# One 130-column product for the high and low parts of the values in three of four output slots, with the two halves added by VectorE

## The chip, the core and the metric

The kernel runs on one core of one Trainium2 chip. The metric is device microseconds of one execution, from the host's view of the device; the core's own span, from the first to the last profiled instruction, is a little shorter. TensorE (PE in the rows; PEld is its weight load) does the matmuls, VectorE (DVE), ScalarE (ACT) and GpSimd (POOL) the elementwise work, SyncE (SP) issues nearly all DMAs. The engines run side by side and wait for each other through semaphores.

## The reference

Attention over 4 batches, 8 heads, 768 positions and head dimension 64, with a block mask of 32 x 32 blocks (neighbours, first and last block, three sampled blocks for each row of blocks), and behind it a two-layer MLP with a mish-like gate:

```python
scores = scale * np.matmul(q, k.transpose(0, 1, 3, 2))      # (4, 8, 768, 768)
scores = np.where(mask, scores, -1e9)
attn = np.exp(scores - np.max(scores, axis=-1, keepdims=True))
attn = attn / (np.sum(attn, axis=-1, keepdims=True) + 1e-09)
x = np.matmul(attn, v)                                       # then (3072, 512)
h = x @ w_in                                                 # (3072, 2048)
g = h * np.tanh(np.where(h > 20.0, h, np.log1p(np.exp(np.minimum(h, 20.0)))))
return g @ w_out                                             # (3072, 512)
```

All is float32 (the weights come as float64). In the kernel most products are float16: a value is split into a high part (its float16 rounding) and a low part (the rest), and a product of two such values is three float16 products, high x high, high x low and low x high.

## The kernel before

A row of blocks has 32 queries. Two neighbouring rows of blocks make a job; the first and the last row of each batch, which see all 768 keys, are a job of one row each ("dense"). So a batch has 13 jobs: 11 of two rows and 2 dense ones, 52 in all. The first batch (jobs 0 to 12) is computed in float32 ("exact"), the other three in float16 parts; the change concerns these 39 jobs alone.

One job goes through these steps, each a task in the code of `attend`:

- S (L657): scores of 32 queries x 4 head pairs against 256 gathered keys for each row and each of two heads (`g`), into PSUM.
- L700, L713, L726: row maximum (DVE), its negative scaled (ACT or DVE), exponential (ACT).
- T (L746): 128 x 128 transposes of the exponentials, four for each group of 256 keys; L763 (ACT) writes their high part and L766 (DVE) their low part, the tile `pp`.
- O (L801): exponentials times values. The values lie in SBUF (`vg`, `v`, `vt`) as 130 columns for each key and head: 64 high parts, a one, 64 low parts, a zero. The 65th column gives the sum of the exponentials. For each row of a job (`w`), each head of a pair (`g`) and each half of the 256 keys (`k`) there are three products: high exponentials x high values and the one (65 columns), high x low values (64 columns), low exponentials x high values (65 columns). Each is four matmuls, one for each head pair, on a tile of 128 rows x 32 columns of the array, which write to the four quarters of the PSUM partitions. All three add up in the same 65 columns of PSUM. The pool `o` has one buffer.
- L824, L825, L827 (DVE, one task): small constant added to the sum, reciprocal, product, into the tile `xs` in SBUF.
- X (L834): `xs` transposed, 128 columns for each row; L852 (ACT) and L855 (DVE) make the high and low part of the MLP's input.

The MLP works on 256 tokens at a time (12 such groups): H (L1033) is `x @ w_in` in pieces of 12 matmuls of 256 columns; L1042 to L1079 on ACT, DVE and POOL make the gate; Y (L1093) is the product with `w_out` in pieces of 6 matmuls of 512 columns.

The order of all engines' instructions is made when the program is built, by `Plan.emit`: a list scheduler that takes each task's written duration (the second argument of `add`), its dependencies, the buffers of each pool and a priority (`key`), and puts the tasks one by one. The MLP's pieces on TensorE have a fixed order and come where nothing else of the attention is due. A task that names a second engine under `also` goes to the one that would end it sooner. The written durations decide the order and nothing else: on the chip the engines run that order and wait for semaphores.

Of the kernel before, what the change touches and what calls it, by code (L numbers as in the profile page):

```python
# [13 lines left out]
AF = mybir.ActivationFunctionType  # L14
ALU = mybir.AluOpType
# [6 lines left out]
PSC = 4096.0  # L22
# [4 lines left out]
             xs=2, hs=3, us=3, g=4, ys=1, kt=1, q=2, ssk=2, ssv=2, ssq=2, sck=2, scv=2, scq=2, iv=2, ns=3, ws=2,  # L27
# [13 lines left out]
class Plan:  # L41
# [10 lines left out]
    def add(self, eng, dur, fn, r=(), w=(), new=(), use=(), key=0.0, lat=0.0, kind=None, port=False, also=()):  # L52

        t = Task({eng: (dur, fn, port), **{e: (d, f, port) for e, d, f in also}}, key, lat, new, kind, len(self.tasks))
        self.tasks.append(t)
        for ring, k in new:
            self.first[k], self.users[k] = t, []
        for k in r:
            t.deps.update(self.writer.get(k, ()))
            self.readers.setdefault(k, []).append(t)  # L60
        for k in w:
            t.deps.update(self.writer.get(k, ()))
            t.deps.update(self.readers.pop(k, ()))
# [122 lines left out]
def attn_mish_kernel(ctx: ExitStack, tc: tile.TileContext, qT, kT, v, sampled, blocks, w_in, w_out, out):  # L186
# [11 lines left out]
    nc = tc.nc  # L198
    P = 128
    B, NPR, D2, S = qT.shape  # L200
    D = D2 // 2
# [15 lines left out]
    VW = 2 * D + 2  # L217
# [7 lines left out]
    exact = lambda b: b == 0  # L225
# [436 lines left out]
    def attend(job):  # L662

        b, i, sus, nt, dense = job["b"], job["i"], job["sus"], job["nt"], job["dense"]
        nsu = len(sus)
        W2 = S - 512
        ks, kmx, kp, ko = ("s", i), ("mx", i), ("pt", i), ("o", i)
# [4 lines left out]
        def s_fn():  # L672
# [15 lines left out]
            r=KT3(b) + [("q", b, t) for t in qts] + (["t in order"] if dense else [(k, su["ng"] % NKG) for su in sus for k in ("kg", "kw")]),  # L688
            w=[ks, ("begun", i), "s in order"] + (k2 if dense else []), new=[("s", ks)] + ([("t", k) for k in k2] if dense else []),
# [18 lines left out]
        def nb_fn(eng):  # L708
            mx, nb = tl[kmx], new(sb, "nb", ("nb", i), [P, 2, 2])
            for w in wq:  # L710
                ns = ns0 if exact(b) else tl["ns", b, sus[w.start]["qb"] // TB]
                if eng == "ACT":
                    nc.scalar.activation(out=nb[:, :, w], in_=mx[:, :, w], func=AF.Copy, scale=ns[:, 1:2])  # L713
                else:
                    nc.vector.tensor_scalar(out=nb[:, :, w], in0=mx[:, :, w], scalar1=ns[:, 1:2], scalar2=None,
                                            op0=ALU.mult)
        add("ACT", 0.25 * len(wq), lambda: nb_fn("ACT"), r=[kmx] + NS, w=[("nb", i)],
            new=[("nb", ("nb", i))], key=45.5 + (0 if b == 0 else -20), also=[("DVE", 0.35 * len(wq), lambda: nb_fn("DVE"))])
# [16 lines left out]
        for n in range(2):  # L735
            add("ACT", 1.7 if dense and n == 0 else 1.15, lambda n=n: ex_fn(n),
                r=[kmx, ("nb", i), ks] + (k2 if dense else []) + NS,
                w=[("p", i, n)], new=[("pt", k) for k in kps] if n == 0 else (), use=kps, key=-1.5 + (-3 if b == 0 else 7))
# [15 lines left out]
        def pp_fn(j, eng):  # L754
            pp_new(j)
            if eng == "ACT":
                nc.scalar.activation(out=tl["p32", i, j], in_=tl["t", i, j], func=AF.Copy)
            else:
                nc.vector.tensor_copy(out=tl["p32", i, j], in_=tl["t", i, j])
# [9 lines left out]
        for j in range(nt):  # L769
            kj = ("t", i, j)  # L770
            add("PE", 0.62 if exact(b) else 0.48, lambda j=j: t_fn(j), r=[("p", i, j // 2 if dense else j)], w=[kj, "t in order"], new=[("t", kj)], use=kps,
                key=-8 + (-40 if b == 0 else 24), lat=0.25, kind=("T", i))
            kpp = ("pp", i, j)
            if exact(b):
                add("ACT", 0.62, lambda j=j: pp_fn(j, "ACT"), r=[kj], w=[("ph", i, j), ("pl", i, j)], use=[kpp],
                    new=[("pp", kpp)], key=-9.5, also=[("DVE", 0.72, lambda j=j: pp_fn(j, "DVE"))])
# [2 lines left out]
            add("DVE", 0.72, lambda j=j: pl_fn(j), r=[kj, ("ph", i, j)], w=[("pl", i, j)], use=[kpp], key=11.5)  # L779

        def o_fn(j):
            if j == 0:
                new(ps["o"], "o", ko, [P, 2, 2, D + 2])
            o, w = tl[ko], 0 if dense else j
            vt = (vg32 if exact(b) else vgs)[sus[w]["ng"] % NVG] if not dense else tl["vt", b, j] if sus[0]["qb"] else tl["v", b, j]
            if exact(b):
                for g in range(2):
                    for k in range(2):
                        for c in range(NPR):
                            cs = slice(c * BS, (c + 1) * BS)  # L790
                            nc.tensor.matmul(  # L791
                                o[cs, w, g, 0:D + 1], tl["p32", i, j][:, k, g, cs], vt[:, k, 2 * c + g],
                                start=j == 0 and g == 0 and k == 0, stop=j == nt - 1 and g == 1 and k == 1)
                return
            hi, lo = tl["ph", i, j], tl["pl", i, j]
            for g in range(2):
                for k in range(2):
                    for n, (p, v0, v1) in enumerate(((hi, 0, D + 1), (hi, D + 1, 2 * D + 1), (lo, 0, D + 1))):
                        for c in range(NPR):
                            cs = slice(c * BS, (c + 1) * BS)  # L800
                            nc.tensor.matmul(  # L801
                                o[cs, w, g, 0:v1 - v0], p[:, k, g, cs], vt[:, k, 2 * c + g, v0:v1],
                                start=j == 0 and g == 0 and k == 0 and n == 0,
                                stop=j == nt - 1 and g == 1 and k == 1 and n == 2)
        def rv(j):
            if not dense:
                return ("vg", sus[j]["ng"] % NVG)
            if sus[0]["qb"]:
                return ("vg", j) if j < NVG else ("vt", b)
            return ("v", b, j)  # L810

        for js in [[j] for j in range(nt)] if i < SPLIT else [list(range(nt))]:
            add("PE", (0.68 if exact(b) else 0.46) * len(js), lambda js=js: [o_fn(j) for j in js],
                r=[k for j in js for k in (("ph", i, j), ("pl", i, j), rv(j))], w=[ko, "o in order"],
                use=[("pp", i, j) for j in js],
                new=[("o", ko)] if js[0] == 0 else (), key=-1 + (-33 if b == 0 else -9), lat=0.25, kind=("O", i))

        def xs_fn():
            o = tl[ko]
            r = new(sb, "r", ("r", i), [P, nsu, 2])  # L820
            if exact(b):
                nc.vector.tensor_scalar(out=r, in0=o[:, 0:nsu, :, D], scalar1=1e-9, scalar2=iv_r, op0=ALU.add, op1=ALU.mult)
            else:
                nc.vector.tensor_scalar(out=r, in0=o[:, 0:nsu, :, D], scalar1=PSC * 1e-9, scalar2=None, op0=ALU.add)  # L824
            nc.vector.reciprocal(out=r, in_=r)  # L825
            xs = new(sb, "xs", ("xs", i), [P, nsu, 2, D])
            nc.vector.tensor_tensor(  # L827
                out=xs, in0=o[:, 0:nsu, :, 0:D], in1=r.unsqueeze(3).to_broadcast([P, nsu, 2, D]), op=ALU.mult)
        add("DVE", 0.8, xs_fn, r=[ko] + ([("sc", "v", b, 0)] if exact(b) else []), w=[("r", i), ("xs", i)], new=[("r", ("r", i)), ("xs", ("xs", i))], key=39.5 + (0 if b == 0 else -27))

        def tx_fn():
            tx = new(ps["t"], "t", ("tx", i), [P, nsu, P])
# [21 lines left out]
        def xl_fn():  # L854
# [3 lines left out]
            new=[("x" + n, ("x" + n, b, t)) for t in fresh for n in "hl"], use=kx, key=-19.5 + (0 if b == 0 else -39))  # L858
# [279 lines left out]
    def open_mlp():  # L1138
# [7 lines left out]
        key=-1025)  # L1146
    load32("k", 0)
    load32("q", 0)
    for j in T3:
        load(0, "v", [j])  # L1150
    add("ACT", 1.0, lambda: which(new), w=["off", "z"],
        new=[("raw", ("z",))], key=-1, lat=6.0)
# [9 lines left out]
    for k in range(NFP):  # L1162
# [3 lines left out]
        key=-3)  # L1166
# [26 lines left out]
    for i, job in enumerate(jobs):  # L1193
        b, o = job["b"], i % JB
# [4 lines left out]
        for su in job["sus"]:  # L1199
# [5 lines left out]
            elif su["qb"]:  # L1205
                fetch_dense(su)
                fresh = jobs[i + 1]["sus"][0]["ng"]
        attend(job)
        if i == LAST:
            add("PE", 0.0, spare.clear, r=["zeros", ("begun", i)], use=[("zeros",)], key=-982)  # L1210
# [27 lines left out]
    at = {"done": 0.0, "next": 0.0, "job": 0, "last": None, "shape": None}  # L1238
# [73 lines left out]
```

## Time and profile before

| | us |
|---|---|
| median of 3 runs | 766.79 (765.13 to 769.03) |
| the profiled execution | 768.72 |
| its span | 766.7 |
| TensorE busy | 733.4 (96%) |
| ScalarE busy | 535.8 (70%) |
| VectorE busy | 504.0 (66%) |
| GpSimd busy | 230.6 (30%) |

The profiled execution is 2.0 us longer than its span and 1.9 us longer than the median. Attention runs until about 642 us; the rest of the span is MLP alone. The steps O of the three float16 batches lie between 203 and 642 us. A row of a timeline merges equal instructions that follow each other; its duration goes to the end of the last one, which overlaps the start of the next row, so that the time that a step takes is read from the start of its row to the start of the next one.

### The profile page before, as it was taken

Reading aid. Unit: us, or ns where it says so; the run is one execution under the profiler, and the core shown is the slowest. Engines: PE = TensorE matmul, PEld = TensorE weight load, DVE = VectorE, ACT = ScalarE, POOL = GpSimd, SP = SyncE. Lnnn points to the kernel's source line nnn. Section 1 sums busy time; section 2 is a strip of 40 time slices with the busy share of each in tenths; the row PEclk is TensorE's granted clock in tenths of the full one; section 3 lists DMA queues with packets and bytes.
Section 4 is the critical chain, followed back from the end, with each engine's and each line's share of the span. In section 5 each row is a group of like instructions: output and inputs, shape, how many; then the busy total and the mean of one; then the engine's idle time right before and its main releaser. Section 6 shows DMA issues by size and latency. Waiting matters only on the chain.

```text
span 766.7 us, 28001 instructions
## 1 busy us (share of the span) xinstructions
PE 733.4 (96%) x11905; PEld 507.3 (66%) x11905; DVE 504.0 (66%) x891; ACT 535.8 (70%) x864; POOL 230.6 (30%) x327
## 2 busy tenths in 40 slices
PE   9777898999999999999999999999999999999998
PEld 3554676766677766677767776766776666666663
DVE  3886897887888748859676676777855454425241
ACT  2556787989887867888797678877864655455650
POOL 2363423585645422514340113234522100000000
PEclk9999999999999999999999999999999999999999
DMA  7987768442346533543363336233233221000000
GB/s 263 363 222 219 232 210 230 147 128 87 106 120 168 160 96 110 170 123 105 103 210 97 94 100 200 84 97 101 71 92 90 96 67 48 15 15 15 15 15 27
DMA packets 55904, 94.07 MB, mean 123 GB/s; under 512 B 8035, under 2 KB 18788, under 8 KB 55780
## 3 DMA queue, kind: packets, MB, share of 16 engines
q1 hardware_dynamic: 55584, 92.03, 40.0%
q8 instruction: 93, 1.52, 0.8%
q14 instruction: 31, 0.25, 0.1%
q10 hardware_dynamic: 196, 0.27, 0.1%
HBM read 79.32 MB, written 12.95 MB: 120 GB/s over the span
## 4 chain that ended last, share of the span: by engine, by line
PE 82%; DMA 9%; DVE 4%; issue 2%; SPq 2%; ACT 1%; ACTq 0%; POOL 0%
PE y L1093 31%; PE h L1033 30%; PE t L746 6%; PE o L801 5%; PE s L657 4%; DMA wr<-in_moe_w_in_dram 3%; DMA vg<-vd 3%; PE tx L834 2%; PE o L791 1%; DMA wor<-in_moe_w_out_dram 1%; DMA kt<-in_k_dram 1%; PE s L647 1%; PE zeros L868 1%; DMA raw_q<-in_q_dram 1%; DVE us L1060 1%
## 5 line engine op out<-in xcount | busy, mean ns | idle before, releaser
L1033 PE MATMUL h<-xh,wi 128*128 128x256 f16 x1536 | 285.3, 274 | 0.0
L1093 PE MATMUL y<-wo,g 128*128 128x512 f16 x1152 | 277.7, 379 | 1.5 <-issue 1.5
L1033 PEld LDWEIGHTS <-wi 128*128 128x128 f16 x2304 | 224.7, 99 | 52.4 <-issue 1.5
L1033 PE MATMUL h<-xl,wi 128*128 128x256 f16 x768 | 210.5, 274 | 0.0
L1093 PEld LDWEIGHTS <-g 128*128 128x128 f16 x1152 | 111.0, 98 | 101.2 <-issue 3.2
L585 POOL COPY kg<-kt 128x256 f16 (+1 forms) x222 | 97.6, 485 | 145.6 <-PE s L657 115.8
L1042 ACT ACTIVATE hs<-h,gsc 128x512 f32<-128x512 f32 x96 | 65.6, 683 | 63.7 <-PE h L1033 62.9
L726 ACT ACTIVATE pt<-s,nb,ns 128x256 f32<-128x256 f32 (+1 forms) x208 | 105.7, 580 | 5.1 <-PE t L746 3.1
L1066 DVE SCALAR_TENSOR_TENSOR hs<-us,hs 128x1024 f32<-128x1024 f32 x48 | 59.6, 1242 | 43.1 <-ACT us L1065 43.1
L700 DVE TENSOR_REDUCE mx<-s 128x4 f32<-128x1024 f32 x44 | 53.7, 1221 | 31.5 <-PE s L657 30.1
L1077 POOL TENSOR_TENSOR g<-hs,g 128x1024 f16<-128x1024 f32 x19 | 42.3, 2229 | 98.9 <-ACT g L1072 60.2
L746 PE MATMUL t<-ident,pt 128*128 128x128 f32 x448 | 69.5, 278 | 2.0 <-ACT pt L726 1.7
L1062 POOL TENSOR_TENSOR us<-us 128x1024 f32<-128x1024 f32 x22 | 43.4, 1971 | 74.7 <-DVE us L1060 72.2
L766 DVE SCALAR_TENSOR_TENSOR pp<-t,pp 128x512 f16<-128x512 f32 x84 | 56.1, 681 | 11.6 <-ACT pp L763 11.5
L763 ACT ACTIVATE pp<-t 128x512 f16<-128x512 f32 x84 | 48.3, 590 | 17.7 <-PE t L746 13.7
L746 PEld LDWEIGHTS t<-ident,pt 128*128 128x128 f32 x448 | 50.8, 141 | 13.9 <-ACT pt L726 3.2
L1056 ACT ACTIVATE us<-hs,hsc 128x1024 f32<-128x1024 f32 x48 | 55.1, 1149 | 1.5
L1064 ACT ACTIVATE us<-us 128x1024 f32<-128x1024 f32 x48 | 50.7, 1056 | 4.9 <-POOL us L1062 4.1
L1065 ACT ACTIVATE us<-us 128x1024 f32<-128x1024 f32 x48 | 50.7, 1056 | 0.7
L1060 DVE TENSOR_SCALAR us<-us 128x1024 f32<-128x1024 f32 x48 | 36.5, 760 | 21.7 <-ACT us L1056 21.5
L801 PEld LDWEIGHTS <-pp 128*32 128x32 f16 x4032 | 37.2, 94 | 13.7 <-issue 12.3
L852 ACT ACTIVATE xh<-tx 128x256 f16<-128x256 f32 (+1 forms) x60 | 19.4, 337 | 31.4 <-PE tx L834 24.8
(194 smaller groups left out, 849.7 us busy)
## 6 DMA issues: line engine op xcount, KB each, us to landing
vg<-vd SPq DMA_DIRECT2D x304, 65.0 KB, 2.3
vg<-vd SPq DMA_DIRECT2D x80, 195.0 KB, 2.9
wr<-in_moe_w_in_dram SPq DMA_DIRECT2D x8, 1024.0 KB, 9.2
wor<-in_moe_w_out_dram SPq DMA_DIRECT2D x16, 512.0 KB, 5.0
vd<-v SPq DMA_DIRECT2D x12, 520.0 KB, 3.4
raw_v<-in_v_dram SPq DMA_DIRECT2D x12, 512.0 KB, 5.7
out_dram<-ys SPq DMA_DIRECT2D x24, 256.0 KB, 2.1
raw_q<-in_q_dram SPq DMA_DIRECT2D x9, 512.0 KB, 5.5
```

The costliest lines, as they stand in the source:

```text
L585: nc.gpsimd.tensor_copy(out=dst, in_=src)
L700: nc.vector.tensor_reduce(out=mx.rearrange("p g w -> p (g w)"), in_=tl[ks].rearrange("p g (w k) -> p (g w) k", k=KT), axis=AX.X, op=ALU.max)
L726: ex = lambda o, x, g, w: nc.scalar.activation(out=o, in_=x, func=AF.Exp, bias=nb[:, g, w:w + 1], scale=ns(w)[:, 0:1])
L746: nc.tensor.transpose(t[:, k, g], src, ident)
L766: nc.vector.scalar_tensor_tensor(out=tl["pl", i, j], in0=tl["t", i, j], scalar=PSC, in1=tl["ph", i, j], op0=ALU.mult, op1=ALU.subtract)
L801: nc.tensor.matmul(o[cs, w, g, 0:v1 - v0], p[:, k, g, cs], vt[:, k, 2 * c + g, v0:v1], start=j == 0 and g == 0 and k == 0 and n == 0, stop ...
L1033: nc.tensor.matmul(h[:, f2].rearrange("p (s q) -> p s q", q=BS), wi[:, fp, w, cc, fs], x[:, :, cc], start=f2 == 0 and k == 0, stop=f2 == 1 ...
L1042: nc.scalar.activation(out=tl[kq][:, 2 * (fp % 2):2 * (fp % 2) + 2], in_=tl[kh], func=AF.Copy, scale=gsc[:, fp:fp + 1])
L1056: nc.scalar.activation(out=new(sb, "us", ku, [P, 4, TT]), in_=hs(), func=AF.Exp, scale=hsc[:, b:b + 1])
L1064: add("ACT", 1.07, lambda: nc.scalar.activation(out=us(), in_=us(), func=AF.Ln, bias=1.0), w=[ku], key=10 + (18 if b == 0 else -12))
L1066: add("DVE", 1.32, lambda: nc.vector.scalar_tensor_tensor(out=hs(), in0=us(), scalar=-0.5, in1=hs(), op0=ALU.add, op1=ALU.mult), r=[ku], w ...
L1093: nc.tensor.matmul(tl[ky], tl["g", b, t, k][:, g, f, q], wo[:, fc, w], start=fc == 0 and n == 0, stop=fc == NFC - 1 and n == 2)
```

## The change

For three of the four (row, head) slots of a job, `m = 2 * w + g` in 0, 1, 2, the products of the high exponentials with the high and with the low values become one matmul of 130 columns. Its output has two runs of 65 columns: slot `m` and slot `m + 4` of a PSUM tile that now has seven slots of 65 columns. The low exponentials x high values still go to slot `m`. The fourth slot, which a dense job has not, keeps its three products. A new task copies slots 4 to 6 to `xs` in SBUF (ACT or DVE), and the task on DVE then adds the first slots to it, multiplies by the reciprocal, and multiplies the fourth slot by itself. The durations that the scheduler is told become 0.42 (was 0.46) for each 256 keys of O, 1.3 (was 0.8) for the task on DVE, and 0.35 (ACT) or 0.3 (DVE) for the copy.

```diff
         def o_fn(j):
-            if j == 0:
+            if j == 0 and exact(b):
                 new(ps["o"], "o", ko, [P, 2, 2, D + 2])
+            elif j == 0:
+                tl[ko] = new(ps["o"], "o", ko, [P, 512], cols=7 * (D + 1)).rearrange("p (s d) -> p s d", d=D + 1)
...
             for g in range(2):
+                m = 2 * w + g
                 for k in range(2):
-                    for n, (p, v0, v1) in enumerate(((hi, 0, D + 1), (hi, D + 1, 2 * D + 1), (lo, 0, D + 1))):
+                    steps = ((hi, 0, VW, slice(m, m + 5, 4)), (lo, 0, D + 1, m)) if m < 3 else (
+                        (hi, 0, D + 1, m), (hi, D + 1, 2 * D + 1, m), (lo, 0, D + 1, m))
+                    for n, (p, v0, v1, at) in enumerate(steps):
                         for c in range(NPR):
                             cs = slice(c * BS, (c + 1) * BS)
+                            x = vt[:, k, 2 * c + g, v0:v1]
+                            if v1 == VW:
+                                x = x.rearrange("p (s d) -> p s d", s=2)
                             nc.tensor.matmul(
-                                o[cs, w, g, 0:v1 - v0], p[:, k, g, cs], vt[:, k, 2 * c + g, v0:v1],
+                                o[cs, at] if v1 == VW else o[cs, at, 0:v1 - v0], p[:, k, g, cs], x,
...
-            add("PE", (0.68 if exact(b) else 0.46) * len(js), lambda js=js: [o_fn(j) for j in js],
+            add("PE", (0.68 if exact(b) else 0.42) * len(js), lambda js=js: [o_fn(j) for j in js],
...
             nc.vector.reciprocal(out=r, in_=r)
+            if not exact(b):
+                xs = tl["xs", i].rearrange("p w g d -> p (w g) d")
+                m = min(2 * nsu, 3)
+                nc.vector.tensor_tensor(out=xs[:, 0:m], in0=o[:, 0:m, 0:D], in1=xs[:, 0:m], op=ALU.add)
+                rb = r.rearrange("p w g -> p (w g)").unsqueeze(2)
+                nc.vector.tensor_tensor(out=xs[:, 0:m], in0=xs[:, 0:m], in1=rb[:, 0:m].to_broadcast([P, m, D]), op=ALU.mult)
+                if m < 2 * nsu:
+                    nc.vector.tensor_tensor(out=xs[:, m:m + 1], in0=o[:, m:m + 1, 0:D], in1=rb[:, m:m + 1].to_broadcast([P, 1, D]), op=ALU.mult)
+                return
...
+            def xc_fn(eng):
+                m = min(2 * nsu, 3)
+                xs = new(sb, "xs", ("xs", i), [P, nsu, 2, D]).rearrange("p w g d -> p (w g) d")[:, 0:m]
+                src = tl[ko][:, 4:4 + m, 0:D]
...
+            add("ACT", 0.35, lambda: xc_fn("ACT"), r=[ko], w=[("xc", i)], new=[("xs", ("xs", i))], key=0.0,
+                also=[("DVE", 0.3, lambda: xc_fn("DVE"))])
-        add("DVE", 0.8, xs_fn, r=[ko] + ([("sc", "v", b, 0)] if exact(b) else []), w=[("r", i), ("xs", i)], new=[("r", ("r", i)), ("xs", ("xs", i))], key=39.5 + (0 if b == 0 else -27))
+        add("DVE", 0.8 if exact(b) else 1.3, xs_fn, r=[ko] + ([] if exact(b) else [("xc", i)]) + ([("sc", "v", b, 0)] if exact(b) else []), w=[("r", i), ("xs", i)], new=[("r", ("r", i))] + ([("xs", ("xs", i))] if exact(b) else []), key=39.5 + (0 if b == 0 else -27))
```

Two places show it in the order of the instructions. On TensorE, in the first step O of the float16 batches, one set of products (`pp` holds the exponentials, `o` is the output), five rows of before:

```order
L801 LDWEIGHTS pp_0_3512
L801 MATMUL o_3642<-v_0_3171,pp_0_3512 32x65
L801 LDWEIGHTS pp_0_3512
L801 MATMUL o_3642<-v_0_3171,pp_0_3512 32x64
L801 LDWEIGHTS pp_0_3512
```

and the same five places of the changed kernel:

```order
L809 LDWEIGHTS pp_0_3512
L809 MATMUL o_3642<-v_0_3171,pp_0_3512 32x2x65
L809 LDWEIGHTS pp_0_3512
L809 MATMUL o_3642<-v_0_3171,pp_0_3512 32x65
L809 LDWEIGHTS pp_0_3512
```

The last matmul of 65 columns has become one of 2 x 65, the 64-column one behind it is gone, and the next is the product of the low exponentials. Of 4032 pairs of weight load and matmul in these steps 2952 stay. Up to this place TensorE's order is the same in both.

On VectorE, around the first step O of a job of two rows (`s` are scores, `mx` their maxima, `kg` gathered keys, `xl` the low part of the MLP's input), before:

```order
L591 COPY kg_110<-kt_2916 128x8x96
L824 TENSOR_SCALAR r_4044<-o_3916 128x4
L825 RECIPROCAL r_4044<-r_4044 128x4
L827 TENSOR_TENSOR xs_4047<-o_3916,r_4044 128x256
L700 TENSOR_REDUCE mx_4143<-s_4060 128x4
L855 TENSOR_TENSOR xl_0_3912<-tx_4056,xh_0_3911 128x256
```

and the same place after the change:

```order
L766 SCALAR_TENSOR_TENSOR pp_1_3802<-t_1_3745,pp_1_3802 128x512
L855 COPY xs_3995<-o_3899 128x192
L832 TENSOR_SCALAR r_4047<-o_3899 128x4
L834 RECIPROCAL r_4047<-r_4047 128x4
L838 TENSOR_TENSOR xs_3995<-o_3899,xs_3995 128x192
L840 TENSOR_TENSOR xs_3995<-xs_3995,r_4047 128x192
L842 TENSOR_TENSOR xs_3995<-o_3899,r_4047 128x64
L1095 SCALAR_TENSOR_TENSOR hs_2_0_3413<-us_2_0_3589,hs_2_0_3413 128x1024
```

Three instructions between O and X have become six here. The copy stands on VectorE in 30 of the 39 jobs and on ScalarE in 9. Since the scheduler put the tasks anew, the order of the other work differs from here on too, on all engines: VectorE does 3 fewer of L1074, 1 fewer of L1079, 1 fewer of L1106 and 4 fewer of L715, which stand on ScalarE or GpSimd instead.

## Rows read from the trace of the kernel before

**Rows 1.** The page, part 1: busy time, share of the span, instructions.
```profile
PE 733.4 (96%) x11905; PEld 507.3 (66%) x11905; DVE 504.0 (66%) x891; ACT 535.8 (70%) x864; POOL 230.6 (30%) x327
```
**Rows 2.** Busy time by stage, with TensorE's granted clock, DMA share and GB/s.
```profile
core 0: us, PE busy (x) PEld busy (x) DVE busy (x) ACT busy (x) POOL busy (x), PEclk, DMA share, GB/s
0.00:203.00 203.00, 180.57 (x2775) 122.82 (x2775) 158.21 (x293) 145.93 (x249) 96.89 (x117) 0.97 0.67 207
203.00:642.00 439.00, 431.90 (x8346) 307.66 (x8345) 301.44 (x550) 330.78 (x551) 133.74 (x211) 1.00 0.40 114
642.00:766.70 124.70, 120.97 (x787) 76.86 (x785) 44.36 (x50) 59.09 (x64) 0.00 (x0) 1.00 0.04 16
```
**Rows 3.** All of TensorE's waits, 203 to 642 us: total, times, longest.
```profile
PE o L801 <- issue: 3.2, 2, 1.7
PE y L1093 <- issue: 1.5, 1, 1.5
PE s L657 <- issue: 1.4, 1, 1.4
PE tp_v L391 <- DVE xl L855: 0.5, 1, 0.5
PE t L746 <- DVE pp L766: 0.2, 1, 0.2
PE tx L834 <- DVE xs L827: 0.2, 1, 0.2
```
**Rows 4.** The weight loads of L801: duration ns min/median/max, first and last start.
```profile
L801 PEld LDWEIGHTS <-pp x4032: 92/93/102, 203.1 to 641.4; 128*32 128x32 f16 x192
```
**Rows 5.** Timeline of TensorE around a step O of two rows: start, duration.
```profile
400.62 1.01 PE L801 MATMUL o<-vg,pp 128*32 128x65 f16 x96
401.56 1.47 PE L1093 MATMUL y<-wo,g 128*128 128x512 f16 x6
402.87 0.27 PE L1033 MATMUL h<-xh,wi 128*128 128x256 f16 x1
...
404.07 0.27 PE L1033 MATMUL h<-xh,wi 128*128 128x256 f16 x1
```
**Rows 6.** The same around a dense step O.
```profile
496.02 1.36 PE L801 MATMUL o<-v,pp 128*32 128x65 f16 x144
497.31 0.55 PE L746 MATMUL t<-ident,pt 128*128 128x128 f32 x3
```
**Rows 7.** L801 alone in 0.30 us of a dense step; instructions under way are counted.
```profile
496.40:496.70 0.30, 0.30 (x62) 0.30 (x47) 1.00 0.67 194
```
**Rows 8.** The same in the step of rows 5, its first and second row of blocks.
```profile
400.80:401.10 0.30, 0.30 (x62) 0.30 (x48) 1.00 0.00 0
401.10:401.40 0.30, 0.30 (x55) 0.30 (x40) 1.00 0.00 0
```
**Rows 9.** Mean ns of one and busy us, by line and shape, whole span.
```profile
L827 DVE TENSOR_TENSOR xs<-o,r 128x256 f32<-128x256 f32 x44 | 18.7, 424 | 1.5
L827 DVE TENSOR_TENSOR xs<-o,r 128x128 f32<-128x128 f32 x8 | 2.3, 291 | 0.3
L759 DVE COPY pp<-t 128x512 f32<-128x512 f32 x7 | 4.8, 688 | 1.7 <-PE t L746 1.7
L852 ACT ACTIVATE xh<-tx 128x256 f16<-128x256 f32 x36 | 13.6, 379 | 19.5 <-PE tx L834 19.2
```
**Rows 10.** Timeline of VectorE behind a step O whose last matmul ended at 414.19 us.
```profile
414.29 0.16 DVE L824 TENSOR_SCALAR r<-o 128x4 f32<-128x4 f32 x1 [2.96 <-PE o L801]
414.49 0.18 DVE L825 RECIPROCAL r<-r 128x4 f32<-128x4 f32 x1
414.70 0.42 DVE L827 TENSOR_TENSOR xs<-o,r 128x256 f32<-128x256 f32 x1
```
**Rows 11.** The step O before it and the X behind it, timeline of TensorE.
```profile
413.18 1.01 PE L801 MATMUL o<-vg,pp 128*32 128x65 f16 x96
...
418.03 0.38 PE L834 MATMUL tx<-ident,xs 128*128 128x128 f32 x2
```

More of the change, by code (lines that the diff above doesn't have):

```diff
@@ L796, in o_fn @@
             for g in range(2):
+                m = 2 * w + g
                 for k in range(2):
-                    for n, (p, v0, v1) in enumerate(((hi, 0, D + 1), (hi, D + 1, 2 * D + 1), (lo, 0, D + 1))):
+                    steps = ((hi, 0, VW, slice(m, m + 5, 4)), (lo, 0, D + 1, m)) if m < 3 else (
+                        (hi, 0, D + 1, m), (hi, D + 1, 2 * D + 1, m), (lo, 0, D + 1, m))
+                    for n, (p, v0, v1, at) in enumerate(steps):
                         for c in range(NPR):
                             cs = slice(c * BS, (c + 1) * BS)
+                            x = vt[:, k, 2 * c + g, v0:v1]
+                            if v1 == VW:
+                                x = x.rearrange("p (s d) -> p s d", s=2)
                             nc.tensor.matmul(
-                                o[cs, w, g, 0:v1 - v0], p[:, k, g, cs], vt[:, k, 2 * c + g, v0:v1],
+                                o[cs, at] if v1 == VW else o[cs, at, 0:v1 - v0], p[:, k, g, cs], x,
                                 start=j == 0 and g == 0 and k == 0 and n == 0,
-                                stop=j == nt - 1 and g == 1 and k == 1 and n == 2)
+                                stop=j == nt - 1 and g == 1 and k == 1 and n == len(steps) - 1)
         def rv(j):
@@ L823, in xs_fn @@
             else:
-                nc.vector.tensor_scalar(out=r, in0=o[:, 0:nsu, :, D], scalar1=PSC * 1e-9, scalar2=None, op0=ALU.add)
+                nc.vector.tensor_scalar(out=r.rearrange("p w g -> p (w g)"), in0=o[:, 0:2 * nsu, D], scalar1=PSC * 1e-9,
+                                        scalar2=None, op0=ALU.add)
             nc.vector.reciprocal(out=r, in_=r)
+            if not exact(b):
[7 more added lines that the diff above has]
+                return
             xs = new(sb, "xs", ("xs", i), [P, nsu, 2, D])
@@ L828, in xs_fn @@
                 out=xs, in0=o[:, 0:nsu, :, 0:D], in1=r.unsqueeze(3).to_broadcast([P, nsu, 2, D]), op=ALU.mult)
-        add("DVE", 0.8, xs_fn, r=[ko] + ([("sc", "v", b, 0)] if exact(b) else []), w=[("r", i), ("xs", i)], new=[("r", ("r", i)), ("xs", ("xs", i))], key=39.5 + (0 if b == 0 else -27))
+        if not exact(b):
+            def xc_fn(eng):
+                m = min(2 * nsu, 3)
+                xs = new(sb, "xs", ("xs", i), [P, nsu, 2, D]).rearrange("p w g d -> p (w g) d")[:, 0:m]
+                src = tl[ko][:, 4:4 + m, 0:D]
+                if eng == "ACT":
+                    nc.scalar.activation(out=xs, in_=src, func=AF.Copy)
+                else:
+                    nc.vector.tensor_copy(out=xs, in_=src)
+            add("ACT", 0.35, lambda: xc_fn("ACT"), r=[ko], w=[("xc", i)], new=[("xs", ("xs", i))], key=0.0,
+                also=[("DVE", 0.3, lambda: xc_fn("DVE"))])
+        add("DVE", 0.8 if exact(b) else 1.3, xs_fn, r=[ko] + ([] if exact(b) else [("xc", i)]) + ([("sc", "v", b, 0)] if exact(b) else []), w=[("r", i), ("xs", i)], new=[("r", ("r", i))] + ([("xs", ("xs", i))] if exact(b) else []), key=39.5 + (0 if b == 0 else -27))
         def tx_fn():
```

## The prediction

> **What bounds the kernel now.** I read the page's first part, then the busy time by stage, then TensorE's waits. The page shows TensorE busy for 96% of the span and no other engine over 70% [rows 1]. The table by stage says where its idle time lies: 22 us before 203 us, 7 us between 203 and 642 us, 4 us in the tail of the MLP [rows 2]. All steps that the change touches lie in the middle stage [rows 4]. There TensorE's granted clock is 1.00, its 2.4 GHz level, and 439.0 - 431.9 = 7.1 us are idle. The list of its waits accounts for them: 3.2 + 1.5 + 1.4 = 6.1 us under "issue", for which the profile names no releaser, in four pieces, and only 0.9 us behind another engine [rows 3]. So between 203 and 642 us the program's time is the sum of what TensorE has to do. A nanosecond taken off a step there comes off the end, unless TensorE has then to wait for something it has not waited for yet. A nanosecond added to VectorE or ScalarE costs nothing until TensorE waits for it.
>
> A busy TensorE says little about what sets its pace, so the step O itself comes next. One of two rows is 96 pairs of weight load and matmul; it starts at 400.62 and the next work at 401.56, so 0.94 us [rows 5]. A dense one is 144 pairs, from 496.02 to 497.31, 1.29 us [rows 6]. What would the columns alone cost? In the MLP, twelve 256-column matmuls start 0.109 us apart (402.87 to 404.07, eleven steps) and six of 512 columns take 1.31 us, 0.218 each [rows 5]: 0.109 us for 256 more columns, 0.43 ns for a column, no fixed part to speak of. Four matmuls on the four column tiles run beside each other, so four of 65 columns would be over in 65 x 0.43 = 28 ns. In the dense step 47 weight loads are under way in a stretch of 0.30 us; each lasts 0.093 us, so these are the starts of 0.393 us: 8.4 ns for a pair, 33 ns for four [rows 4, 7]. The pairs come more slowly than their columns would be streamed: the step is paced by the number of pairs. In the second row of blocks it is slower still, 0.393 us / 40 = 9.8 ns, against 8.2 ns in the first [rows 8].
>
> **What the change does, part by part.**
>
> *Fewer pairs on TensorE.* A set (one head, one half of the keys) has 12 pairs before. Merged it has 8, of which four have 130 columns: 55 ns of streaming, and four have 65: 28 ns, 83 ns together. The eight pairs at 8.4 ns need 67 ns, so a merged set is bound by its columns, not by its pairs, and costs 83 ns. Before it cost 12 x 8.4 = 101 ns in a first row of blocks or a dense step, and 12 x 9.8 = 118 ns in a second row.
> - Two rows (33 jobs): four sets of the first row, 4 x (101 - 83) = 72 ns; two of the second row's four, 2 x (118 - 83) = 70 ns; the fourth slot's two sets stay. Together 0.14 us a job, 33 x 0.14 = 4.7 us.
> - Dense (6 jobs): twelve sets, 12 x 18 = 0.21 us, 6 x 0.21 = 1.3 us.
> - Sum: 6.0 us less on TensorE, from 1080 pairs removed (270 merged sets x 4).
>
> No row shows a matmul of 130 columns on a tile of 32 columns, or one whose output has two runs, so its price is bounded. At best the columns are hidden and only the pairs count: a merged set saves 4 x 8.4 = 34 ns, 270 x 34 = 9.1 us. At worst from the rows, a merged four costs as much as the two fours it replaces: nothing is saved. I take the streaming price, 6.0 us, since the MLP's rows carry it over to twice the columns.
>
> The Trainium skill has a rule against this. "TensorEngine Tiling (Array Packing)", section "Instruction Overhead", says that each matmul has about 60 cycles of overhead and that one of 1 column lasts as long as one of 60. By that rule a 65-column matmul lies above its floor already and merging two saves nothing; the sum would be 0 in place of 6.0 us. The 8.4 ns between pairs speaks against taking that floor for four tiles side by side; the rule's result stands below as a rival.
>
> *More on VectorE and ScalarE.* Behind a step O of two rows VectorE had 0.16, 0.18 and 0.42 us [rows 10]. Now the product of 256 columns gives way to an addition and a product of 192 columns each and a product of 64. A line through 291 ns at 128 columns and 424 at 256 [rows 9] gives 358 and 225 ns: 358 + 358 + 225 - 424 = 0.52 us more. In a dense job one more of 128 columns, 0.29 us. In sum 33 x 0.52 + 6 x 0.29 = 18.9 us. The copy of 192 columns costs about 0.36 us on VectorE (the copy of 512 takes 688 ns [rows 9], less 320 x 1.04 ns), 30 x 0.36 = 10.8 us, and under 0.38 us on ScalarE [rows 9], 3 us for nine. In the middle stage VectorE is busy for 301 of 439 us and ScalarE for 331 [rows 2]; VectorE comes to about 331, less some 6 us for the nine instructions that the new order gives to others. Both keep 100 us of idle time, which hides all this; I cost the load itself at nothing.
>
> *A longer way from O to X.* That cover fails where TensorE reaches X before `xs` is ready. Before, `xs` is ready 0.94 us after the last matmul of O ends: 413.18 + 1.01 = 414.19 to 414.70 + 0.42 = 415.12, and X starts at 418.03 [rows 10, 11]. With starts as they follow each other in that row (0.04 to 0.06 us between instructions) the new chain is 0.10 + 0.40 (copy) + 0.20 + 0.21 + 0.42 + 0.42 + 0.23 = 1.98 us. Queued behind a waiting X are all later pieces of the MLP and all later jobs. What covers it is the order: counted in it, with 1.3 us for six matmuls of Y or twelve of H [rows 5] and the streamed columns for other steps, between an O and its X stand on average about 3.6 us of TensorE work before and 4.5 us after the change. The shortest cover after is twelve matmuls of H and a score step of 48 on eight tiles, 1.3 + 48 x 0.109 / 8 = 2.0 us; before, four places had 1.3 us or less. The scheduler was told of the longer chain and has moved the X back. The only wait of X on `xs` in the middle stage was 0.2 us in all [rows 3], with a cover at its shortest about equal to the chain, as it is again. I take 0.5 us for such waits now; the bounds are nothing and the whole added 1.04 us at each of 39 places, 41 us, which the counted cover excludes. The `o` buffer is held about 1 us longer; the next O is never less than 5 us of TensorE work behind in the new order, so this costs nothing.
>
> *The reordered rest.* Up to 203 us TensorE's order is the same. After it the same steps stand in other places; behind the last O the same amount of MLP work is left as before (456 matmuls of H, 330 of Y), so the tail does not change. I take nothing for this, with 2 us either way.
>
> **Sum.** -6.0 + 0.5 = -5.5 us. The profiled execution took 768.72 us, 2.0 more than its span; it would come to 763.2. It lies 1.9 us over the median of 766.79, from which the same gain gives 761.3 us, 0.7% faster. About 0.5%, 3.8 us, is what a measurement of this kernel can tell from no change.
>
> **The rivals.**
> - *The longer chain eats it.* TensorE waits for `xs` or for tasks pushed back on VectorE, some 0.1 us at each of 39 jobs: 4 us back, 765. For it: the chain doubles and the cover at its shortest is as long as the chain. Against it: the cover grew on average too, and TensorE's waits on other engines now come to 0.9 us [rows 3].
> - *No gain from merging.* Time follows the columns, 195 for each set and tile as before, or the 130-column four costs two fours: only the 0.5 us of waits is left, some 767. The pace of pairs [rows 7, 8] speaks against it.
> - *The split output is slow.* Each 130-column matmul writes two runs 260 columns apart, and slots begin at odd multiples of 65 words. If the writing took twice the streaming time, a merged set would cost 2 x 55 + 28 = 138 ns; against 101 ns at 204 sets and 118 at 66 that is 204 x 37 + 66 x 20 = 8.9 us more, with the waits 776, slower. It decides from the point where a merged four costs 55 + 6.0 us / 270 = 77 ns, 1.4 times its streaming. No output of before has two runs, so no row speaks for or against. "PSUM — Partial Sum Buffer", section "Specifications (TRN2)", of the Trainium skill does: it names 8-byte lines and says that an access pattern that isn't contiguous slows matmuls significantly. No run here shows that.
> - *More than forecast.* Fewer pairs also mean fewer of the 1.4 to 1.7 us pieces under "issue" [rows 3]; two gone would give 758.
>
> **How the numbers follow.** Forecast 0.52 (its own range 759 to 763.5), chain 0.20, no gain 0.12, split output 0.09, more 0.07. Faster by over 0.5% means under 762.95: nearly all of the forecast's chance (0.48) and the last one (0.07), with 0.01 of the chain's: 0.56. Within 0.5%: 0.04 of the forecast's, most of the chain's (0.17) and of the no-gain case (0.11): 0.32. Slower: the split output and what the chain and the new order could cost beyond 4 us: 0.12. The range 757 to 768 leaves out the slower case and the end of the chain's, about 0.12, and little below.
>
> **What would show it.** O of two rows should take about 0.80 us from its start to the next work, a dense one about 1.08. Four 130-column matmuls should start 55 to 60 ns before the next four; 70 or more would be the split output. TensorE's waits on DVE `xs` should stay under 1 us in sum between the first float16 O and the last X. VectorE should be busy some 24 us longer in all. I am wrong if O is not shorter by 0.1 us, or if the list of waits shows several us before X.

## The result, and the profile after

The changed kernel takes 756.79 us (median of 4 runs, 756.11 to 757.21) against 766.5 us (4 runs); the ratio is 0.987, with a 95% interval of 0.984 to 0.990. It is 1.3% faster where 0.7% was forecast, and 0.2 us below the range's lower end. The profiled execution took 756.11 us with a span of 754.3. Busy time on the page after (columns as in [rows 1]):

```profile
PE 731.3 (97%) x10825; PEld 504.9 (67%) x10825; DVE 528.5 (70%) x984; ACT 540.8 (72%) x883; POOL 241.1 (32%) x326
```

1080 pairs are gone from TensorE and VectorE is busy 24.5 us longer. TensorE's busy time fell by only 2 us over the span: it is 4.3 us less in the middle stage (431.2 and 426.9 us) and 2.1 us more before it (180.7 and 182.8). So the gain has to be read from the steps and the waits. The steps O lie in these stretches, the first and the last start of the products in `v` and `vg`:

```profile
L809 PE MATMUL o<-vg,pp x2568: 191/196/234, 208.0 to 629.1; 128*32 128x65 f16 x108, 128*32 128x130 f16 x69, 128*32 128x64 f16 x21
L809 PE MATMUL o<-v,pp x288: 192/208/233, 200.0 to 498.6; 128*32 128x130 f16 x72, 128*32 128x65 f16 x72
```

I call the time from the first start of a float16 O to the last one the middle stage. It was 641.4 - 203.1 = 438.3 us [rows 4] and is 629.1 - 200.0 = 429.1 us: 9.2 us less, which is nearly all. The first O comes 3.1 us earlier in this execution, though TensorE's order up to it is the same; a second execution of the kernel before had it at 198.7 us (below), so this is chance.

**Two terms make the 9.2 us.** The first is the step O itself. Timelines of TensorE after the change, a step of two rows and a dense one, each with the row that follows it:

```profile
399.44 0.91 PE L809 MATMUL o<-vg,pp 128*32 128x130 f16 x72
400.28 0.44 PE L746 MATMUL t<-ident,pt 128*128 128x128 f32 x2
```
```profile
497.56 1.25 PE L809 MATMUL o<-v,pp 128*32 128x130 f16 x96
498.74 0.44 PE L863 MATMUL tx<-ident,xs 128*128 128x128 f32 x2
```

From start to next start 0.84 us, where it was 0.94 [rows 5], and 1.18, where it was 1.29 [rows 6]. 33 x 0.10 + 6 x 0.11 = 4.0 us. (All 39 steps together, without the pieces named below, take 39.2 us before and 35.0 after.) The second is the waits of TensorE, all of them between 198 and 631 us (total, times, longest):

```profile
PE o L809 <- issue: 1.6, 1, 1.6
PE tx L863 <- DVE xs L840: 0.2, 1, 0.2
PE tx L863 <- DVE pp L766: 0.2, 1, 0.2
```

Of four pieces named "issue", 6.1 us [rows 3], one of 1.6 us is left: 4.5 us. The waits on other engines went from 0.9 to 0.4 us. 4.0 + 4.5 + 0.5 = 9.0 of the 9.2 us.

**What an "issue" piece is.** The list names no releaser. Here is one of before in the timeline of TensorE:

```profile
516.17 0.60 PE L746 MATMUL t<-ident,pt 128*128 128x128 f32 x4
516.70 0.85 PE L657 MATMUL s<-kg,q 64*32 64x256 f16 x48
517.48 0.66 PE L746 MATMUL t<-ident,pt 128*128 128x128 f32 x4
518.06 0.67 PE L801 MATMUL o<-vg,pp 128*32 128x65 f16 x61
520.45 0.46 PE L801 MATMUL o<-vg,pp 128*32 128x65 f16 x35 [1.72 <-issue]
```

TensorE stops in the middle of a step, after 61 of its 96 pairs, and the profile shows nothing that it waits for. What stands ahead is dense: 4 + 48 + 4 + 61 = 117 pairs in 2.6 us. It is not the densest stretch: from 203.1 us on there are 196 pairs in 2.5 us, and no stop. Part 3 of the page has a queue "q8 instruction", which one easily passes over. Before and after:

```profile
q8 instruction: 93, 1.52, 0.8%
```
```profile
q8 instruction: 85, 1.39, 0.8%
```

93 packets for the 2 x 11905 matmuls and weight loads of TensorE are one for each 256; 85 for 2 x 10825 are one for 255. So these packets (16,384 bytes in the DMA records) follow TensorE's instructions. In those records one begins at 518.04 us, just ahead of the stop, and ends at 519.10; TensorE goes on 1.35 us later. The other three pieces of before end 1.4 to 1.5 us after such a packet too. The theory for the experiments, A: TensorE's instructions arrive in blocks of 256, and where O and S follow each other closely it has used up its stock before the next block is there. The experiments below test it, and a count of the instructions ahead of each stop settles where a stop can lie.

### The profile page after: what moved, and what is told of

It reads as the page before. It is cut to its first block, busy times and chain, and to the rows that moved or that the text cites. A ratio compares the mean times of both kernels' runs of the same rounds, so it can differ in the third digit from the quotient of the medians.

```text
span 754.3 us, 25951 instructions
## 1 busy us (share of the span) xinstructions
PE 731.3 (97%) x10825; PEld 504.9 (67%) x10825; DVE 528.5 (70%) x984; ACT 540.8 (72%) x883; POOL 241.1 (32%) x326
## 4 chain that ended last, share of the span: by engine, by line
PE 85%; DMA 8%; DVE 4%; SPq 2%; issue 1%; ACT 0%; ACTq 0%; DVEq 0%
PE y L1122 32%; PE h L1062 31%; PE t L746 6%; PE o L809 4%; PE s L657 4%; DMA wr<-in_moe_w_in_dram 3%; DMA vg<-vd 3%; PE tx L863 2%; PE o L793 2%; PE s L647 1%; PE zeros L897 1%; DMA kt<-in_k_dram 1%; SPq L610 1%; DVE mx L700 1%; DMA vd<-z 1%
## 5 line engine op out<-in xcount | busy, mean ns | idle before, releaser
L1091 POOL TENSOR_TENSOR us<-us 128x1024 f32<-128x1024 f32 x26 | 51.5, 1980 | 76.4 <-DVE us L1089 75.0
L1106 POOL TENSOR_TENSOR g<-hs,g 128x1024 f16<-128x1024 f32 x20 | 45.4, 2268 | 87.6 <-DVE g L1103 36.3
L746 PE MATMUL t<-ident,pt 128*128 128x128 f32 x448 | 70.6, 282 | 0.1
L746 PEld LDWEIGHTS t<-ident,pt 128*128 128x128 f32 x448 | 52.5, 143 | 13.3 <-issue 3.2
L897 PE MATMUL zeros<-z 128*128 128x512 f16 x139 | 37.6, 415 | 3.7 <-issue 2.0
L809 PEld LDWEIGHTS <-pp 128*32 128x32 f16 x2952 | 32.6, 97 | 12.4 <-issue 11.1
```

What stands on the lines that cost most here:

```text
L746: nc.tensor.transpose(t[:, k, g], src, ident)
L809: nc.tensor.matmul(o[cs, at] if v1 == VW else o[cs, at, 0:v1 - v0], p[:, k, g, cs], x, start=j == 0 and g == 0 and k == 0 and n == 0, stop ...
L1091: add("POOL", 2.0, lambda: nc.gpsimd.tensor_tensor(out=us(), in0=us(), in1=us(), op=ALU.mult), w=[ku], port=True, key=47 + (56 if b == 0 e ...
```

## Experiments

Each column is read from the run's profile: q8 packets, the "issue" waits of TensorE in the middle stage in us with their number, its length, and the median of the run's times. The times of a group were taken together, with the kernel before beside them.

| kernel | q8 | issue | stage | median |
|---|---|---|---|---|
| before | 93 | 6.1 (4) | 438.3 | 766.5 |
| changed | 85 | 1.6 (1) | 429.1 | 756.8 |
| before_again | 93 | 5.6 (4) | 438.0 | 764.0, one run |
| before_shift64 | 94 | 6.7 (7) | 439.8 | 768.5 |
| three_products | 93 | 9.2 (7) | 443.8 | 770.3 |
| after_shift64 | 86 | 0 | 428.2 | 756.7 |
| (before in this group) | | | | 766.7 |
| y_split | 94 | 0.4 (1) | 430.4 | 759.7 |
| copy_twice | 85 | 0 | 429.0 | 757.8 |
| after_shift32 | 85 | 0 | 428.3 | 754.5 |
| after_shift96 | 86 | 0.2 (1) | 428.6 | 755.9 |
| (before in this group) | | | | 766.2 |
| after_again | 85 | 1.3 (1) | 428.8 | 757.0 |
| after_shift32_again | 85 | 0 | 428.2 | 755.1 |
| before_drop | 85 | 0.5 (1) | 423.3 | 751.6 |
| before_shift32 | 94 | 4.0 (5), and 1.6 by another name | 438.3 | 767.1 |
| (before in this group) | | | | 768.0 |

**The kernel before once more.** No edit.

> The kernel before once more, to see what of its profile repeats. Theory A (TensorE's instructions come in blocks of 256, and the pieces named issue are places where dense runs of short pairs use them up faster than the next block arrives; the place is fixed by the program): the same four pieces of about 1.5 us in the middle stage, near 466, 498, 518 and 615 us, after a shift by what the start took. Theory B (they are chance): other places or another number, from 0 to 8. The time until the first float16 O, 203.1 us before and 200.0 in the changed kernel although the order up to there is the same: if it is chance it should come out between 199 and 204 us here.

Its waits of TensorE, and the piece that answers to the one shown:

```profile
PE o L801 <- issue: 2.7, 2, 1.5
PE s L657 <- issue: 1.7, 1, 1.7
PE y L1093 <- issue: 1.2, 1, 1.2
```
```profile
513.92 0.67 PE L801 MATMUL o<-vg,pp 128*32 128x65 f16 x61
515.76 0.43 PE L801 MATMUL o<-vg,pp 128*32 128x65 f16 x32 [1.17 <-issue]
```

(This view ends at 516 us, inside the step, so that its last row shows 32 of the 35 pairs left.)

Four pieces on the same lines, and this one after the same 61 pairs, 4.1 us earlier because the first O came at 198.7 us, 0.3 us below what was expected. The place belongs to the program; the start does not keep its time.

**Three products again.** The reordered kernel without the merge:

```diff
-steps = ((hi, 0, VW, slice(m, m + 5, 4)), (lo, 0, D + 1, m)) if m < 3 else (
-    (hi, 0, D + 1, m), (hi, D + 1, 2 * D + 1, m), (lo, 0, D + 1, m))
+steps = ((hi, 0, D + 1, m), (hi, D + 1, 2 * D + 1, m + 4 if m < 3 else m), (lo, 0, D + 1, m))
```

> The changed kernel with three products everywhere again (65, 64 and 65 columns; the middle one goes to slots 4 to 6): order, copy, addition and slots as changed, 4032 pairs instead of 2952. Theory A (pairs: the shorter O and, beside it, fewer blocks of 256 instructions to wait for): O of two rows back to 0.94 us, 93 blocks, 2 to 6 pieces named issue in the middle stage, 764 to 768 us. Theory B (the new order of the work gave what O did not): only the 4 us of O come back, 760 to 762 us, with no more than one issue piece.

770.3 us, ratio to before 1.005 (1.002 to 1.008): above the range of A, and far from B. Its issue pieces, and the longest of them:

```profile
PE s L657 <- issue: 4.3, 2, 3.2
PE o L808 <- issue: 3.3, 2, 2.0
PE h L1061 <- issue: 1.0, 2, 0.7
PE t L746 <- issue: 0.6, 1, 0.6
```
```profile
253.07 1.01 PE L808 MATMUL o<-vg,pp 128*32 128x65 f16 x96
...
255.43 0.83 PE L657 MATMUL s<-kg,q 64*32 64x256 f16 x42
259.49 0.30 PE L657 MATMUL s<-kg,q 64*32 64x256 f16 x6 [3.24 <-issue]
```

The new order and VectorE's additions by themselves are worth less than nothing; the merge is worth 13.5 us in this order by the medians. The profiled execution of this kernel took 774.5 us, 4.2 over its median, so its parts are compared by the stage, 14.7 us longer than in the changed kernel: 4 us are the steps O and 7.6 us issue pieces. After the stop that ended at 423.9 us TensorE's granted clock was 0.67 in the mean from 425 to 430 us, a part of them at the lower level of 1.2 GHz, where the kernel before has 1.00; that takes about 1.7 us of the rest.

**Moving the blocks.** The first 32, 64 or 96 of the 139 zero matmuls near the start are cut into two of half the columns, in `zeros`:

```diff
     def zeros(n):
         for _ in range(n if spare else 0):
-            nc.tensor.matmul(spare[0].rearrange("p (n q) -> p n q", q=P), z16, z16.unsqueeze(1).to_broadcast([P, 4, P]),
-                             start=True, stop=True)
+            halves[0] += 1
+            for c in range(2 if halves[0] <= 64 else 1):
+                w = 2 if halves[0] <= 64 else 4
+                nc.tensor.matmul(spare[0].rearrange("p (n q) -> p n q", q=P)[:, c * w:c * w + w], z16,
+                                 z16.unsqueeze(1).to_broadcast([P, w, P]), start=True, stop=True)
+
+    halves = [0]
```

> The kernel before with the first 64 of its zero matmuls (512 columns each, put in to keep TensorE busy while it waits for the first DMAs) cut into two of 256 columns: the same columns and order, 128 more instructions near the start, so that every later block of 256 begins half a block earlier in the work. Theory A: the issue pieces of the middle stage move to other places and their number changes (0 to 7), and the time follows at 1.5 us for each: 766.5 + 1.5 x (number - 4), within 1.5. Theory B (pieces belong to the work at those places or to DMA traffic): the same four places, 766.5 within 1.

> The kernel before with the first 32 zero matmuls cut in two: 64 more instructions near the start. Theory A: 2 to 6 issue pieces in the middle stage at places that differ from those of the kernel before and of its other shift, 764 to 769 us: no place of the blocks rids the order of before of them, since two shifts had four each. If it has 0 or 1, the four pieces were an unlucky place of the blocks, and the gain of the change from them would be luck: 760 to 762 us.

> The same cut in the changed kernel. Theory A: its one issue piece at 261 us moves or goes, others may come (0 to 4), 756.8 + 1.5 x (number - 1), within 1.5. Theory B: one piece at 261 us, 756.8 within 1.

> The changed kernel with the first 32 zero matmuls cut in two: every later block of 256 instructions begins 64 instructions earlier in the work. Theory A: the middle stage has 0 to 3 issue pieces at places that differ from 261 us, and its length from the first float16 O to the end of the last one is 427.7 us (429.3 less the one piece of 1.6) plus 1.5 us for each; 755 to 760 us in all. Theory B (something else set 261 us): one piece at 261 us.

> The same with 96 of the 139 zero matmuls cut in two, 192 instructions. Theory A as for 64 instructions: 0 to 3 issue pieces at other places, the middle stage 427.7 us plus 1.5 us for each, 755 to 760 us. Theory B: one piece at 261 us.

In the kernel before the pieces moved and did not go. With 64 matmuls cut, the long ones lie at 205.6, 266.9, 350.8 and 394.5 us, and none at 461 to 466, 494 to 498, 514 to 518 or 611 to 615 us, where both profiles of before had theirs:

```profile
PE o L801 <- issue: 2.7, 2, 1.4
PE h L1038 <- issue: 2.1, 2, 1.8
PE s L657 <- issue: 1.4, 1, 1.4
PE y L1098 <- issue: 0.5, 2, 0.3
```

By A's sum seven pieces would have given 771 us; 768.5 came, since three of the seven lasted only 0.2 to 0.3 us. With 32 cut there are 4.0 us of them, and 767.1 us in place of 768.0, no difference. The stage is as long as before all the same, and one more wait says why:

```profile
PE t L746 <- ACT us L1070: 1.6, 1, 1.6
```

The transposes L746 do not read `us`; TensorE goes on here 1.3 us after the end of a q8 packet, at a count of instructions that all the issue pieces share (next paragraph). So this is one more of them under another name, and three places of the blocks had 6.1, 6.7 and some 5.5 us: the loss stays with the many pairs, its places do not. In the changed kernel three shifts have 0 to 0.2 us; the 261 us piece is gone in each, and the stage is 428.2 to 428.6 us, where A's sum had 427.7. That is 0.5 to 0.9 us less for a piece of 1.6, since X then waits longer for VectorE (0.2 us in the changed kernel):

```profile
PE tx L863 <- DVE pp L766: 0.8, 2, 0.6
```

So a price of 1.5 us for each piece is too simple. With 64 cut TensorE also stops more often near the start, in both kernels.

**Where the stops lie.** The traces let one count TensorE's instructions ahead of each stop: matmuls, weight loads, and the semaphore and drain instructions of its sequencer, in the order of their starts. For the stop shown above there are 2 x 8975 + 162 = 18,112 = 70 x 256 + 192. The other three of before stand at 62, 67 and 84 x 256 + 192, the one of the changed kernel at 31 x 256 + 192. So it is in all 14 profiles: each of the 32 issue pieces of the middle stage begins 192 or 193 instructions behind a multiple of 256, and ends 1.2 to 1.7 us after the end of a q8 packet. No other wait of TensorE in this stage stands at that count, but for the 1.6 us by another name. With 32 matmuls cut, two of the stops are those of blocks 67 and 84 again, 32 pairs earlier in the work. That TensorE stops where one block of 256 ends is thus shown, and that it waits there for the next block follows from the packet, which ends shortly ahead of every resumption. It fits that no two of these packets begin less than 3.3 us apart in any of the profiles, while a step O uses 256 instructions (128 pairs at 8.4 ns) in 1.1 us. At most boundaries the block is there in time, in dense places too; what makes the one or the other packet late stays open.

**More instructions outside the dense runs.** Each 512-column matmul of Y in two halves, in `moe_y`:

```diff
-                    nc.tensor.matmul(tl[ky], tl["g", b, t, k][:, g, f, q], wo[:, fc, w],
-                                     start=fc == 0 and n == 0, stop=fc == NFC - 1 and n == 2)
+                    for hf in (slice(0, DM // 2), slice(DM // 2, DM)):
+                        nc.tensor.matmul(tl[ky][:, hf], tl["g", b, t, k][:, g, f, q], wo[:, fc, w, hf],
+                                         start=fc == 0 and n == 0 and hf.start == 0, stop=fc == NFC - 1 and n == 2 and hf.start > 0)
```

> The changed kernel with each 512-column matmul of the MLP's second product cut into two of 256 columns: 1152 pairs more, the same columns, spread over the MLP's steps and not in the dense runs of attention. Theory A1 (TensorE runs out of instructions only where dense runs, O and S, stand close together): about 94 blocks of 256, as many as the kernel before, yet 0 to 3 issue pieces in the middle stage; 756.8 to 761 us. Theory A2 (the mere number of blocks decides): 4 to 6 pieces again, 761.5 to 766 us. O of two rows stays at 0.84 us in both.

94 packets, one more than in the kernel before, and no piece over 0.4 us; all of TensorE's waits in the stage:

```profile
PE tx L863 <- DVE pp L766: 0.6, 1, 0.6
PE tx L863 <- issue: 0.4, 1, 0.4
PE tx L863 <- DVE xs L840: 0.2, 1, 0.2
```

A1 holds: what counts is how fast the dense runs use instructions, not how many there are. The 2.9 us against the changed kernel are not issue pieces. The stage is 1.3 us longer with 1.2 us less of them, so other work takes some 2.5 us more; that this is the price of the cut itself is likely, and no run separates it.

**Fewer pairs in the old order.** The kernel before without the product of high exponentials and low values in slots 0 to 2 (the loop then runs over `steps`):

```diff
-                    for n, (p, v0, v1) in enumerate(((hi, 0, D + 1), (hi, D + 1, 2 * D + 1), (lo, 0, D + 1))):
+                    steps = ((hi, 0, D + 1), (hi, D + 1, 2 * D + 1), (lo, 0, D + 1))
+                    if 2 * w + g < 3:
+                        steps = steps[0:1] + steps[2:3]
+                    for n, (p, v0, v1) in enumerate(steps):
...
```

> The kernel before, in its own order and with its own work on VectorE, with the product of high exponentials and low values left out for the three slots that the change merges (so that part of the output is missing): 2952 pairs as in the changed kernel, and 64 columns fewer in each such set. Theory A (fewer pairs in dense runs take the issue pieces away, whatever the order): 85 blocks, 0 to 2 pieces in the middle stage instead of 4; O of two rows about 0.70 us and dense about 0.90, so 10 us from O and 3 to 6 us from the pieces: 750 to 754 us. Theory B (the new order took them away): 4 pieces, 755 to 757 us.

751.6 us, ratio 0.980 (0.978 to 0.982). A step of two rows takes 0.74 us:

```profile
233.87 0.81 PE L804 MATMUL o<-vg,pp 128*32 128x65 f16 x72
234.61 0.55 PE L746 MATMUL t<-ident,pt 128*128 128x128 f32 x3
```

and the issue pieces are down to 0.5 us with the order of before. Fewer pairs take most of them away, in either order.

**A longer chain and more work for VectorE.** The copy of slots 4 to 6 a second time, ahead of the addition, which the scheduler does not know of:

```diff
+                nc.vector.tensor_copy(out=xs[:, 0:m], in_=o[:, 4:4 + m, 0:D])
```

> The changed kernel with the copy of slots 4 to 6 done once more by VectorE ahead of the addition (the scheduler isn't told): 39 instructions of 0.29 to 0.36 us, 13.5 us more for VectorE, and a chain from O to X that is 0.4 us longer. Theory of the prediction (VectorE's load is hidden, the chain just covered): waits of X on xs grow by 0 to 3 us; 756.8 to 760 us. Rival (VectorE's load is no longer hidden): 39 x 0.4 = 15 us or more, 770 us.

757.8 us. VectorE is busy 539.4 us, 10.9 more than in the changed kernel, and X waits 1.6 us in all instead of 0.4:

```profile
PE tx L864 <- DVE pp L766: 1.4, 3, 0.8
PE tx L864 <- DVE xs L841: 0.2, 1, 0.2
```

X waits for `xs` no longer than in the changed kernel. Of the 1.2 us more behind `pp`, a wait of 0.5 us at 266 us (0.6 in the shifts) comes wherever the stop at 261 us is gone, and one of 0.75 us at 363 us in this run alone. VectorE's load is hidden, and the order's cover nearly holds even for 0.4 us more. TensorE's instructions are those of the changed kernel, yet the piece at 261 us is not there: in the changed kernel the packet began at 260.01 us, 1.0 us ahead of the stop, and here at 257.86, 4.4 us ahead of the same instruction. The count says where a stop can come; whether the block is in time there also hangs on other things of the execution.

**The changed kernel beside its shift by 32.**

> The changed kernel once more, beside the next one on the same chip, and a second profile. If its single issue piece at 261 us is fixed by the program it is there again; the repeat of the added copy, whose TensorE instructions are the same, had none, so I now expect 0 or 1 there, and 756 to 757.5 us.

> The changed kernel with the first 32 zero matmuls cut in two, again. If the 2.3 us that it was faster belong to where its blocks begin, 754 to 755.5 us, at least 1 us under the changed kernel of the same call; if they were chance, the two within 0.7 us.

The one piece is at 260.1 us again (1.3 us). 756.97 us (6 runs, 754.45 to 761.5) against 755.14 (5 runs, 754.19 to 755.91), after 756.79 against 754.53 in the groups before. The shifted kernel has the lower median both times, by 1.8 and 2.3 us, and no stop in the middle stage; its ratio to before is 0.984 (0.982 to 0.985), that of the changed kernel 0.987 (0.984 to 0.990). The intervals overlap, and its middle stage is shorter by 0.7 to 0.8 us only, so that it beats the changed kernel is likely and not shown. Against the kernel before it is 1.6% faster.

## Why the prediction was wrong

- **The bound.** Right. In the middle stage what TensorE does and waits for made the time, and 9.0 of its 9.2 us are accounted for in these two alone.
- **Fewer pairs.** The mechanism was right, the term too large: 4.0 us, not 6.0. A merged set costs more than its 83 ns of streaming, as seen in a dense step after the change:

```profile
497.80:498.10 0.30, 0.30 (x44) 0.30 (x36) 1.00 0.22 56
498.10:498.40 0.30, 0.30 (x44) 0.30 (x36) 1.00 0.70 132
```

  36 weight loads under way are 0.393 / 36 = 10.9 ns for a pair, 87 ns for eight. The other error is what the pairs cost before. I applied the steady 8.4 ns from the middle of a dense step to all its pairs, but a step starts faster: before, the first 36 went by in 0.28 us.

```profile
495.90:496.30 0.40, 0.28 (x36) 0.28 (x39) 1.00 0.11 21
```

  7.8 ns for a pair, so a set at the start of a step cost about 94 ns, not 101, and merging saved little there. In a step of two rows the first 36 pairs are half of the merged sets (three of six).
- **The issue pieces.** This is the step that failed. I read them, 6.1 us, put them into the account of TensorE's idle time, and then left them out of the sum as something that does not change; the gain of two of them stood only as a rival with a chance of 0.07. They are the larger half of the gain: 4.5 us against 4.0. The runs showed in their place that TensorE stops where a block of 256 instructions comes late. The three products in the new order (9.2 us of pieces) and the dropped product in the old one (0.5 us) show that fewer pairs in the dense runs take them away.
- **VectorE and ScalarE.** Right: 24.5 us more on VectorE against some 24 predicted, 5.0 on ScalarE against 3, and TensorE's waits on VectorE fell from 0.9 to 0.4 us. That VectorE came out so exactly is luck (last section).
- **The chain to X.** Right that it is covered; the 0.5 us was too much. X waits 0.4 us in all, 0.2 of them for `xs`, as before.
- **The reordered rest.** I took nothing for it. With the merge undone the new order was 0.5% slower than the old one, mostly through issue pieces, so it did not bring the gain.
- **The split output.** This rival was wrong. At 87 ns for a merged set there is at most 4 ns over streaming for two runs and odd slots together, where the rival needed 138. In that step the four 130-column matmuls start 56 to 67 ns before the next four (median 59); 70 or more would have been the rival's sign. The rule of the Trainium skill in "PSUM — Partial Sum Buffer", section "Specifications (TRN2)", that an access pattern which isn't contiguous slows matmuls significantly, does not show in outputs of two runs of 65 columns.
- **No gain from merging.** This rival was wrong too. By the rule of the Trainium skill in "TensorEngine Tiling (Array Packing)", section "Instruction Overhead", as the prediction applied it, the step would have stayed at 0.94 us; it fell to 0.84.

## What to carry to other kernels

When a bound engine has idle pieces that no other engine ends, look at the instruction packets of the page's part 3 and at what stands ahead of each stop: short instructions in dense runs can have a second price, and an edit that cuts their number can be worth more than its busy time. A stop that repeats after the same instruction in two profiles, and moves when a few instructions are added far ahead of it, points to supply; that all stops stand at the same count modulo the packet's instructions confirms it, and finds a stop that the profile puts down to another engine. Take the pace of a burst from its start and its middle separately, and undo one part in the new order before crediting the order.

## What was not expected of the hardware

The multiplication L840, which reads and writes SBUF alone, has a median of 358 ns and a longest of 1940 ns:

```profile
L840 DVE TENSOR_TENSOR xs<-xs,r x39: 292/358/1940, 202.5 to 631.4; 128x192 f32<-128x192 f32 x33, 128x128 f32<-128x128 f32 x6
L838 DVE TENSOR_TENSOR xs<-o,xs 128x192 f32<-128x192 f32 x33 | 10.8, 326 | 0.0
```

The addition L838 of the same size, with one input in PSUM, has a mean of 326 ns. The nine longest of L840, 0.84 to 1.94 us, all began while GpSimd was in a two-input instruction over 128 x 1024 elements, and ended 0.15 to 0.22 us after that one did, by the timelines of the two engines. L840 took 23.7 us in all where 13.6 was counted; other instructions of VectorE took less than counted. The scheduler is not told that this task can be held up by GpSimd. X waited for `xs` 0.2 us in all, so it cost the end next to nothing here. The addition L838, with its one input in PSUM, began 12 times while GpSimd was in such an instruction and never took more than 328 ns.
